# Another group spilled through DRAM, sums of squares by transfers, and two merged VectorE operations in a gated linear attention with a mixture of experts

## The chip, the core and the metric

The kernel runs on one core of one Trainium2 chip. A core has TensorE (PE, matrix products, with its weight loads listed as PEld), VectorE (DVE), ScalarE (ACT), GpSimd (POOL) and SyncE (SP), each with an instruction stream of its own that is worked off in order; they meet at semaphores. Transfers are issued from SP's queue or from GpSimd's and are carried out by 16 DMA engines. The metric is the device time of one execution in microseconds (us). Lower is better.

## The reference

A linear attention with complex decay per channel (4 batches, 8 heads, 768 positions, 48 channels), followed by a layer of 8 experts of which each token uses at most one.

```python
mag = np.sqrt(a_re * a_re + a_im * a_im)
scale = np.minimum(mag, 0.999) / (mag + 1e-06)
a_re_n, a_im_n = (a_re * scale, a_im * scale)
for t in range(S):
    ar, ai = (a_re_n[:, :, t, :, None], a_im_n[:, :, t, :, None])
    new_re = ar * S_re - ai * S_im
    new_im = ar * S_im + ai * S_re
    S_re, S_im = (new_re + kv, new_im)          # kv = k[t] outer v[t]
    y[:, :, t] = np.einsum('bhd,bhde->bhe', q[:, :, t], S_re)
...
do_compute = x @ w_skip > 0                     # x: y as 3072 tokens of 384
e_idx = np.argmax(xc @ w_gate, axis=1)          # gate_w: softmax at e_idx
h = np.maximum(xc[mask] @ w1[e], 0.0)
y[mask] = gate_w[mask, None] * (h @ w2[e])
out[do_compute] = xc + y
```

## The kernel before, in words

**Tiling.** The 768 positions are 6 chunks of 128, taken as 3 groups of two. Within a chunk, products of the decay factors run outwards from the middle, backwards in one half and forwards in the other, so that 128 partitions hold (half, chunk, batch and head) and a group needs 64 steps and one at the end. The state of a step, `W`, is a complex product over 48 channels. A group is 8 pieces of 8 steps.

**The recurrence** (`chain`) takes two VectorE operations a step: `X` (L371), the four real products, and the next `W` (L380). Each depends on the one before, and other VectorE work is placed between them.

**A gate** (`gate`, with `scale`) prepares the factors of one piece, two pieces ahead. `ain` holds the imaginary part in column 0, the real part in column 1 and the negated imaginary part in column 2. ScalarE squares the two parts (L258), VectorE adds them (L262), ScalarE makes the scale `t` by logarithm and exponential (L263 to L267, with one VectorE operation, L266). Then VectorE multiplies the imaginary part by `t` and a sign that is -1 on the second half of the partitions (L316), ScalarE writes the negated copy (L321), and VectorE multiplies the real part by `t` (L324). GpSimd sets the few rows at a group's ends.

**A piece is consumed** (`consume`): ScalarE squares `W` (L438), VectorE forms `nw`, a query or key times `W` (L443); the two squares are added by two TensorE products with the identity into a bank of PSUM (L452, tile `sw`), or on VectorE in the last piece of a group (L457); ScalarE takes logarithm and exponential (L459, L460), VectorE refines the reciprocal (L462, L464), applies it (L467) and forms `iw` (L470). In groups that stay on the chip, TensorE transposes `nw` and `iw` (L533) and ScalarE copies the result into `qk` (L540), 16 transposes and 8 copies a piece. `keep` (L492) sends what is needed in natural layout to DRAM (`kq`), from GpSimd's queue: half of it for a group that stays, all of it for the group that is spilled. The last piece of the kernel goes through `final` instead.

**The spilled group** is group 1 (`spilled`). Its transposes are not made in `consume`; each of its units loads keys and queries from `kq` (`nat`, L503; for the others only keys, L506) and `turn` transposes them, 16 transposes (L518) and 4 copies (L520).

**A unit** (`unit_at`, `unit`) is the attention of one chunk and one batch, eight units a group: products of keys and queries (L590, tiles `pa`, two of one bank each), the mask on VectorE (L612, one operation a bank), the state between chunks (L625 to L663), the output products (L667, L670), their transposition (L675), and the scores of the router. The next unit's L590 is issued in the middle of a unit, before its output products. Units of group g run during the recurrence of group g+1; those of group 2 run after it.

**Order.** `Order` is a planner that fixes the program order: it steps generators by priority (units, router, consume, gates, weights) between the steps of the recurrence, with costs and due times of its own. A unit may start only at a given step (`PACE`), a piece of the recurrence only when the piece three before it is consumed, and the pieces of group 2 behind the first only after 8 units, since `qk` has two buffers a group and group 2 takes those of group 0. The scheduler below it works with simulated times; `issue_after` pins the masks behind a step of the recurrence.

**The end.** Router and scatter (L739) bring the tokens of each expert together in DRAM (`xs`); then eight experts run on TensorE, each with two layers in split precision (L1000 to L1028).

Of the kernel before, what the change touches and what calls it, by code (L numbers as in the profile page):

```python
# [9 lines left out]
F32 = mybir.dt.float32  # L10
# [3 lines left out]
AF = mybir.ActivationFunctionType  # L14
ALU = mybir.AluOpType
AX = mybir.AxisListType
PSUM = bass.MemoryType.PSUM
DRAM = bass.MemoryType.DRAM

B, H, S, D = 4, 8, 768, 48  # L20
DM = H * D
BH = B * H
C = 128
HC = 64
NCH = S // C
NG = NCH // 2
# [73 lines left out]
def vt(n, f=1.0):  # L100
    return (n / f + 65) / 0.96
# [8 lines left out]
class Kern:  # L110
# [12 lines left out]
    def consts(self, ctx):  # L123
# [26 lines left out]
        self.sgn = col[:, 0:1]  # L150
        g.memset(self.sgn[0:64], 1.0)
        g.memset(self.sgn[64:128], -1.0)
# [149 lines left out]
    def gate(self, g, p):  # L302
        nc = self.nc
        V, A = nc.vector, nc.scalar
        n = LP + (1 if p == NP - 1 else 0)
        i = g * NP + p
        if i == 0:
            self.load_a(0)
        if i + 1 < NPC:
            self.load_a(i + 1)  # L310
        ain = self.ain[i]
        last = i == NPC - 1
        t = yield from (self.scale_last if last else self.scale)(i, n, ain)
        N = n * D
        o = self.order
        V.scalar_tensor_tensor(ain[:, :, 0], ain[:, :, 0], self.sgn, t, ALU.mult, ALU.mult)  # L316
        if p == 0:
            nc.gpsimd.memset(ain[0:64, 0, 0], 0.0)
        if n > LP:
            nc.gpsimd.memset(ain[64:128, LP, 0], 0.0)  # L320
        A.activation(ain[:, :, 2], ain[:, :, 0], AF.Copy, scale=-1.0)  # L321
        self.ready[i] = o.act(N, 1, o.t + vt(N))
        yield vt(N), 0
        V.tensor_tensor(ain[:, :, 1], ain[:, :, 1], t, ALU.mult)  # L324
        if p == 0:
            nc.gpsimd.memset(ain[0:64, 0, 1], 1.0)
        if n > LP:
            nc.gpsimd.memset(ain[64:128, LP, 1], 1.0)
        yield vt(N), 0
        self.gates_done = i + 1  # L330
# [10 lines left out]
    def chain(self, g):  # L341
        V = self.nc.vector
        qk = None
        if not self.spilled(g):
            qk = [self.qkp.tile([96, BH, 4, HC], F32, name=f"qk_{g}_{cc}", tag="qk") for cc in range(2)]
# [43 lines left out]
    def consumers(self):  # L389
        while self.cons_done < NPC:  # L390
            g, u = divmod(self.cons_done, NP)
            if self.cq and (self.spilled(g) or u < 1 or self.units_done >= (g - 1) * 2 * B):
                yield from self.consume(*self.cq.pop(0))
            else:
                yield 0, 100

        self.rctx.close()
        self.m0 = self.pool(self.mctx, "m0", side="right")
        self.mr = self.pool(self.mctx, "mr", 2, side="right")
        self.t2 = self.pool(self.mctx, "t2", side="right")  # L400
        self.order.add(P_WEIGHTS, self.weights(0, self.m0), 3000)
# [30 lines left out]
    def consume(self, g, i, W, num, inv, jb, qk, wl):  # L432
# [16 lines left out]
        if wl is None:  # L449
            sw = self.ps_w.tile([128, LP, D], F32, name=f"sw_{i}", tag="sw")  # L450
            for c in range(2):
                nc.tensor.matmul(sw, self.ident, ws[:, :, c], start=(c == 0), stop=(c == 1))  # L452
            o.pe(1300, ts)
            cost = 0.0
        else:
            sw = w2
            V.tensor_tensor(w2, w2, r0, ALU.add)  # L457
            cost = vt(N)
# [12 lines left out]
        tq = self.trans(i, iw, 2, 1, jb, qk, vt(2 * N)) + 5000  # L471
# [12 lines left out]
    def spilled(self, g):  # L484

        return g == 1
# [8 lines left out]
    def nat(self, c, b):  # L495

        if c >= 2 * (NG - 1):
            return
        g, cc = divmod(c, 2)
        t = self.nats[c, b] = self.un.tile([C, H, 2, 2 * D], F32, name=f"nat_{c}_{b}", tag="nat")  # L500
        r = cc * BH + b * H
        if self.spilled(g):
            self.nc.sync.dma_start(t.rearrange("p h q d -> p (h q) d"),  # L503
                                   self.kq[g][r:r + H].rearrange("h q s d -> s (h q) d"))
        else:
            self.nc.sync.dma_start(t[:, :, 0], self.kq[g][r:r + H, 0].rearrange("h s d -> s h d"))  # L506

    def turn(self, c, b):
# [3 lines left out]
        qk = self.un.tile([96, H, 4, HC], F32, name=f"qkT_{c}_{b}", tag="qkT")  # L512
# [65 lines left out]
    def unit_at(self, c, b):  # L578
# [9 lines left out]
        pa = [self.ps_at.tile([128, 4, C], F32, name=f"pa_{c}_{b}_{hh}", tag="pa") for hh in range(2)]  # L588
        for h in range(H):
            nc.tensor.matmul(pa[h // 4][:, h % 4], KT(h), QT(h), start=True, stop=True)  # L590
# [8 lines left out]
    def unit(self, c, b):  # L599
# [9 lines left out]
        for hh in range(2):  # L609

            with self.tc.issue_after(self.cins):
                V.tensor_tensor(at[:, hh * 4:hh * 4 + 4], pa[hh],  # L612
                                self.mask.rearrange("p (o t) -> p o t", o=1).to_broadcast([128, 4, C]), ALU.mult)
            yield o.wait(vt(512), 0 if hh == 0 or c == 0 else self.rx_t)
# [76 lines left out]
        nx = c * B + b + 2  # L691
# [12 lines left out]
    def units(self, g):  # L704
        self.nat(2 * g, 0)
        self.nat(2 * g, 1)
# [172 lines left out]
    def attention(self):  # L879
        with ExitStack() as ctx:  # L880
# [4 lines left out]
            self.qkp, self.un, self.st = P("qk", 2), P("un", 2), P("st")  # L885
            self.ps_tp, self.ps_at = P("ps_tp", 2, space=PSUM), P("ps_at", 2, space=PSUM)
# [359 lines left out]
```

## Time and profile before

| | |
|---|---|
| median of 3 runs | 538.61 us (535.48 to 540.12) |
| profiled execution | 543.87 us |
| its span, first to last instruction | 542.2 us |
| mean granted clock of TensorE | 0.887 |
| HBM read, written | 61.84 MB, 25.21 MB |

The profile is of one execution, and its time is outside the range of the three timed runs. A row of a group of instructions gives line, engine, operation, written and read tiles, shape and count; behind the first bar the busy time in us and the mean of one in ns; behind the second the idle time of the engine just before them and what ended it. A row of a stretch gives its length, then busy us and instructions of each engine, TensorE's granted clock, the DMA share and GB/s. A row of waits gives who waited for whom, us in total, times, and the longest. A row in order of time gives start, duration, engine, line and shape, and how many like it are merged. A row of a transfer gives KB each and the median us from issue to landing. Busy time of TensorE is not time at its peak, and idle time of an engine that does not bound a stage costs nothing.

### The profile page before, as it was taken

The numbers are of one execution on the slowest core, as the hardware profiler recorded it, in microseconds if no ns is written. First come the engines' busy times: TensorE is split into PE (matmuls) and PEld (weight loads), VectorE is DVE, ScalarE is ACT, GpSimd is POOL, SyncE is SP. The second block draws the span as 40 slices with busy tenths as digits, with TensorE's granted clock in tenths as the row PEclk, the third lists the DMA queues.
The fourth block names the chain that finished last, engine by engine and source line by source line (L and its number), as shares of the span: only waits on it lengthen the run. The fifth ranks groups of instructions, "written<-read, shape, count | busy, mean of one in ns | idle before, by whom it ended". The sixth has DMA issues, their size and how long they took to land. (4 is left out here: it accounts for less than half of the span.)

```text
span 542.2 us, 10042 instructions
## 1 busy us (share of the span) xinstructions
PE 430.7 (79%) x3253; PEld 376.9 (70%) x3253; DVE 412.1 (76%) x1139; ACT 291.8 (54%) x658; POOL 88.3 (16%) x158
## 2 busy tenths in 40 slices
PE   0256446579989322899999998999998999999994
PEld 0134324479866201788778888998988999999994
DVE  2988999965999989789889847689469566866621
ACT  3657657714655554587778673332266454654410
POOL 4011011101132444000000300202112001120111
PEclk9966876667999765799999996799999999999998
DMA  4558777787988867858644325534659568666300
GB/s 85 113 113 179 176 151 169 159 163 178 230 196 195 197 152 168 186 113 194 135 112 110 96 67 179 145 113 119 219 175 312 189 209 273 182 196 226 105 20 28
DMA packets 160523, 85.72 MB, mean 158 GB/s; under 512 B 134491, under 2 KB 154463, under 8 KB 160464
## 3 DMA queue, kind: packets, MB, share of 16 engines
q1 hardware_dynamic: 155216, 70.93, 51.7%
q0 software_dynamic: 5248, 14.07, 9.6%
q8 instruction: 28, 0.46, 0.3%
q14 instruction: 31, 0.25, 0.1%
HBM read 61.84 MB, written 25.21 MB: 161 GB/s over the span
## 5 line engine op out<-in xcount | busy, mean ns | idle before, releaser
L452 PE MATMUL sw<-ws,ident 128*128 128x384 f32 x84 | 44.3, 664 | 37.9 <-ACT ws L438 37.9
L371 DVE TENSOR_TENSOR X<-W,ain 128x192 f32<-128x192 f32 x192 | 67.7, 352 | 2.9
L936 DVE TENSOR_TENSOR l<-r,h 128x768 fp32r<-128x768 f32 (+1 forms) x56 | 58.0, 1069 | 13.3 <-ACT h L935 13.2
L935 ACT CAST h<-r 128x768 fp32r<-128x768 f32 (+1 forms) x56 | 49.7, 925 | 17.6 <-DMA r<-in_moe_w_dram 12.7
L452 PEld LDWEIGHTS sw<-ws,ident 128*128 128x128 f32 x84 | 19.5, 257 | 50.6 <-issue 27.1
L1000 PE MATMUL ph<-xh,h 128*128 128x256 f32 x192 | 53.0, 282 | 0.6 <-issue 0.6
L1000 PE MATMUL ph<-xh,l 128*128 128x256 f32 x192 | 53.2, 282 | 0.0
L1002 ACT ACTIVATE hh<-ph 128x256 fp32r<-128x256 f32 x64 | 23.7, 382 | 53.8 <-PE ph L1000 53.8
L612 DVE TENSOR_TENSOR at<-pa,mask 128x512 f32<-128x512 f32 x48 | 32.7, 685 | 25.1 <-PE pa L590 21.4
L380 DVE TENSOR_TENSOR W<-X 128x96 f32<-128x96 f32 x192 | 48.7, 254 | 3.4
L1000 PE MATMUL ph<-xl,h 128*128 128x256 f32 x192 | 51.0, 281 | 0.0
L533 PE MATMUL tp<-ident,iw 128*96 128x128 f32 x128 | 23.6, 331 | 33.6 <-DVE iw L470 33.3
L1003 DVE SCALAR_TENSOR_TENSOR hl<-ph,hh 128x256 fp32r<-128x256 f32 x64 | 25.6, 418 | 29.2 <-ACT hh L1002 29.2
L540 ACT COPY qk<-tp 96x256 f32<-96x256 f32 x128 | 39.8, 369 | 11.4 <-PE tp L533 10.9
L1023 PE MATMUL po<-h,hh 128*128 128x384 f32 x128 | 43.8, 342 | 0.0
L739 POOL DMA_INDIRECT xs<-xa,sl x24 | 29.1, 1212 | 88.8 <-DVE l L936 20.5
L533 PEld LDWEIGHTS tp<-ident,iw 128*96 128x96 f32 x128 | 17.1, 151 | 37.9 <-issue 30.6
L1024 PE MATMUL po<-l,hh 128*128 128x384 f32 x128 | 43.3, 338 | 0.0
L667 PE MATMUL py<-at,vt 128*64 128x128 f32 x384 | 42.5, 298 | 0.0
L590 PE MATMUL pa<-qk 96*128 96x128 f32 x256 | 41.3, 316 | 1.0 <-DVE at L612 0.9
L1025 PE MATMUL po<-h,hl 128*128 128x384 f32 x128 | 39.5, 337 | 0.0
L590 PEld LDWEIGHTS pa<-qk 96*128 96x128 f32 x256 | 36.9, 222 | 3.2 <-PE py L670 1.1
(225 smaller groups left out, 1077.2 us busy)
## 6 DMA issues: line engine op xcount, KB each, us to landing
r<-in_moe_w_dram SPq DMA_DIRECT2D x24, 512.0 KB, 5.4
r<-in_moe_w_dram SPq DMA_DIRECT2D x32, 384.0 KB, 4.2
nat<-kq SPq DMA_DIRECT2D x8, 768.0 KB, 5.5
kq<-nw POOLq DMA_DIRECT2D x24, 192.0 KB, 3.4
kq<-iw POOLq DMA_DIRECT2D x24, 192.0 KB, 2.9
vt<-in_v_dram SPq DMA_DIRECT2D x24, 192.0 KB, 2.8
out_dram<-xa SPq DMA_DIRECT2D x24, 192.0 KB, 2.1
ain<-in_a_re_dram SPq DMA_DIRECT2D x90, 48.0 KB, 2.9
```

What stands on the lines that cost most here:

```text
L371: V.tensor_tensor(X, prev.unsqueeze(1).to_broadcast([128, 2, 2, D]), windows(ain[:, j]), ALU.mult)
L380: self.cins = V.tensor_tensor(W[:, j, ::-1], X[:, :, 0], X[:, :, 1], ALU.add).ins
L452: nc.tensor.matmul(sw, self.ident, ws[:, :, c], start=(c == 0), stop=(c == 1))
L533: nc.tensor.transpose(tp[:, jj], src[:, s * 4 + jj], self.ident)
L540: nc.scalar.copy(o, tp[:, :, :, cc].rearrange("p j s b -> p b s j"))
L590: nc.tensor.matmul(pa[h // 4][:, h % 4], KT(h), QT(h), start=True, stop=True)
L667: PE.matmul(py[j * 64:j * 64 + 64, hp], vt_[:, 2 * hp + j], at[:, 2 * hp + j], start=True, stop=(c == 0))
L935: nc.scalar.copy(hi[:, ks], raw)
L936: nc.vector.tensor_tensor(lo[:, ks], raw, hi[:, ks], ALU.subtract)
L1000: pe = PE.matmul(ph, w[:, k, js], x[:, k], start=(n == 0), stop=(n == len(terms) - 1))
L1023: PE.matmul(po, hh[:, j, sl], w2h[:, j], start=(j == 0), stop=False)
L1024: PE.matmul(po, hh[:, j, sl], w2l[:, j], start=False, stop=False)
```

## The change

Group 0 is spilled instead of group 1. The `qk` pool has three buffers: one for group 0, which holds its loads (`nat`) and turned tiles as parts of one area, and two for each of groups 1 and 2 in turn; a piece of group 2 behind the first is consumed only after 12 units. For group 1, the keys are loaded into one buffer, one unit ahead instead of two. Units of a group that is not spilled may start 5 us earlier in the planner's time.

In groups 1 and 2 the two squares are added by an accumulating transfer within SBUF, from GpSimd's queue, in place of TensorE's two products (and VectorE's sum in the last piece of group 1). Group 0 keeps TensorE's sums.

In a gate, ScalarE first negates the imaginary part on the second half of the partitions, in place; then one VectorE operation multiplies both parts by `t`. The negated copy follows it. In a unit, `pa` is one tile of two banks and the mask one operation; the pool has one buffer of it instead of two.

```diff
+        A.activation(ain[64:128, :, 0], ain[64:128, :, 0], AF.Copy, scale=-1.0)
+        o = self.order
+        o.act(n * D)
         t = yield from (self.scale_last if last else self.scale)(i, n, ain)
-        V.scalar_tensor_tensor(ain[:, :, 0], ain[:, :, 0], self.sgn, t, ALU.mult, ALU.mult)
+        V.tensor_tensor(ain[:, :, 0:2], ain[:, :, 0:2], t.unsqueeze(2).to_broadcast([128, n, 2, D]), ALU.mult)
...
-        A.activation(ain[:, :, 2], ain[:, :, 0], AF.Copy, scale=-1.0)
-        V.tensor_tensor(ain[:, :, 1], ain[:, :, 1], t, ALU.mult)
+        A.activation(ain[:, :, 2], ain[:, :, 0], AF.Copy, scale=-1.0)
...
-            qk = [self.qkp.tile([96, BH, 4, HC], F32, name=f"qk_{g}_{cc}", tag="qk") for cc in range(2)]
+        qk = [self.qkp.tile([128, BH * 4 * HC], F32, name=f"qk_{g}_{cc}", tag="qk")
+              for cc in range(1 if self.spilled(g) else 2)]
+        if self.spilled(g):
+            self.area, qk = qk[0], None
...
-            if self.cq and (self.spilled(g) or u < 1 or self.units_done >= (g - 1) * 2 * B):
+            if self.cq and (g < NG - 1 or u < 1 or self.units_done >= 3 * B):
...
-        if wl is None:
+        if g:
+            sw = w2
+            nc.gpsimd.dma_start(w2, r0, accum_op=ALU.add)
+            ts += 4000
+            cost = 0.0
+        elif wl is None:
...
-        tq = self.trans(i, iw, 2, 1, jb, qk, vt(2 * N)) + 5000
+        tq = self.trans(i, iw, 2, 1, jb, qk, vt(2 * N)) + 5000 * self.spilled(g)
...
-        return g == 1
+        return g == 0
...
-        t = self.nats[c, b] = self.un.tile([C, H, 2, 2 * D], F32, name=f"nat_{c}_{b}", tag="nat")
         if self.spilled(g):
+            t = self.part(c, b, 0, H * 4 * D).rearrange("p (h q d) -> p h q d", h=H, q=2)
...
         else:
+            t = self.un.tile([C, H, 1, 2 * D], F32, name=f"kt_{c}_{b}", tag="kt", bufs=1)
...
+    def part(self, c, b, o, n):
+        o += (c * B + b) % 2 * n
+        return self.area[:, o:o + n]
...
-        qk = self.un.tile([96, H, 4, HC], F32, name=f"qkT_{c}_{b}", tag="qkT")
+        qk = self.part(c, b, 2 * H * 4 * D, H * 4 * HC)[0:96].rearrange("p (h k t) -> p h k t", h=H, k=4)
...
-        pa = [self.ps_at.tile([128, 4, C], F32, name=f"pa_{c}_{b}_{hh}", tag="pa") for hh in range(2)]
+        pa = self.ps_at.tile([128, H, C], F32, name=f"pa_{c}_{b}", tag="pa")
...
+            V.tensor_tensor(at, pa, self.mask.rearrange("p (o t) -> p o t", o=1).to_broadcast([128, H, C]), ALU.mult)
...
-        nx = c * B + b + 2
+        nx = c * B + b + (2 if self.spilled(c // 2) else 1)
...
-            self.qkp, self.un, self.st = P("qk", 2), P("un", 2), P("st")
-            self.ps_tp, self.ps_at = P("ps_tp", 2, space=PSUM), P("ps_at", 2, space=PSUM)
+            self.qkp, self.un, self.st = P("qk", 3), P("un", 2), P("st")
+            self.ps_tp, self.ps_at = P("ps_tp", 2, space=PSUM), P("ps_at", 1, space=PSUM)
```

More of the change, by code (lines that the diff above doesn't have):

```diff
@@ L149, in consts @@
         col = cst.tile([128, 8], F32, name="col")
-        self.sgn = col[:, 0:1]
-        g.memset(self.sgn[0:64], 1.0)
-        g.memset(self.sgn[64:128], -1.0)
         self.lnb = col[:, 1:2]
@@ L320, in gate @@
             nc.gpsimd.memset(ain[64:128, LP, 0], 0.0)
[L321 to L324, printed above, removed]
+            nc.gpsimd.memset(ain[64:128, LP, 1], 1.0)
         if p == 0:
             nc.gpsimd.memset(ain[0:64, 0, 1], 1.0)
-        if n > LP:
-            nc.gpsimd.memset(ain[64:128, LP, 1], 1.0)
-        yield vt(N), 0
+        A.activation(ain[:, :, 2], ain[:, :, 0], AF.Copy, scale=-1.0)
+        self.ready[i] = o.act(N, 1, o.t + vt(2 * N))
+        yield vt(2 * N), 0
         self.gates_done = i + 1
@@ L342, in chain @@
         V = self.nc.vector
-        qk = None
-        if not self.spilled(g):
-            qk = [self.qkp.tile([96, BH, 4, HC], F32, name=f"qk_{g}_{cc}", tag="qk") for cc in range(2)]
+        qk = [self.qkp.tile([128, BH * 4 * HC], F32, name=f"qk_{g}_{cc}", tag="qk")
+              for cc in range(1 if self.spilled(g) else 2)]
+        if self.spilled(g):
+            self.area, qk = qk[0], None
+        else:
+            qk = [t[0:96].rearrange("p (h k t) -> p h k t", h=BH, k=4) for t in qk]
         self.QK[g] = qk
@@ L587, in unit_at @@
         nc.sync.dma_start(vt_[:, :, 0:D], self.v3[b * H:b * H + H, c * C:c * C + C, :].rearrange("h s d -> s h d"))
-        pa = [self.ps_at.tile([128, 4, C], F32, name=f"pa_{c}_{b}_{hh}", tag="pa") for hh in range(2)]
+        pa = self.ps_at.tile([128, H, C], F32, name=f"pa_{c}_{b}", tag="pa")
         for h in range(H):
-            nc.tensor.matmul(pa[h // 4][:, h % 4], KT(h), QT(h), start=True, stop=True)
+            nc.tensor.matmul(pa[:, h], KT(h), QT(h), start=True, stop=True)
         self.pa[c, b] = pa
@@ L608, in unit @@
         pa = self.pa.pop((c, b))
[L609 to L614, printed above, removed]
+        with self.tc.issue_after(self.cins):
+            V.tensor_tensor(at, pa, self.mask.rearrange("p (o t) -> p o t", o=1).to_broadcast([128, H, C]), ALU.mult)
+        yield o.wait(vt(1024), 0 if c == 0 else self.rx_t)
         late = self.last(c)
@@ L705, in units @@
         self.nat(2 * g, 0)
-        self.nat(2 * g, 1)
+        if self.spilled(g):
+            self.nat(2 * g, 1)
         self.unit_at(2 * g, 0)
```

2 lines of the change are left out of this document (1 added, 1 removed).

## The prediction

> **What bounds the kernel now.** I read the page first, then the busy time by stage, then the waits of VectorE, and last single instructions in order of time. The page's chain of waits is of no use here (it stops after two pieces, 0.1% of the span), so the bound is read stage by stage. I cut the span where the recurrence of a group ends: the first step starts at 12.2, the last piece's sum on VectorE (L457) marks the ends of groups 0 and 1 at about 95 and 203.7, and the last step ends at about 311. From 311 to 325 the last transposes run, then eight late units to 384.6, then the experts.
>
> ```profile
> span 542.2 us, 10042 instructions
> L371 DVE TENSOR_TENSOR X<-W,ain x192: 343/351/360, 12.2 to 309.9; 128x192 f32<-128x192 f32 x192
> 94.51 0.55 DVE L457 TENSOR_TENSOR ws<-ws 128x384 f32<-128x384 f32 x1
> 203.53 0.55 DVE L457 TENSOR_TENSOR ws<-ws 128x384 f32<-128x384 f32 x1
> core 0: us, PE busy (x) PEld busy (x) DVE busy (x) ACT busy (x) POOL busy (x), PEclk, DMA share, GB/s
> 12.20:95.00 82.80, 40.64 (x144) 26.85 (x145) 75.34 (x201) 54.50 (x137) 10.26 (x20) 0.75 0.70 149
> 95.00:203.70 108.70, 76.53 (x582) 62.24 (x580) 92.92 (x273) 56.14 (x132) 27.46 (x44) 0.80 0.80 184
> 203.70:311.00 107.30, 96.61 (x771) 77.49 (x773) 93.74 (x262) 74.19 (x181) 10.62 (x14) 0.90 0.62 140
> 311.00:325.00 14.00, 13.31 (x134) 11.52 (x130) 6.71 (x24) 10.52 (x33) 1.18 (x2) 1.00 0.25 65
> 325.00:384.60 59.60, 57.54 (x584) 54.19 (x585) 47.17 (x209) 19.69 (x40) 9.54 (x10) 0.89 0.50 147
> 384.60:542.20 157.60, 146.08 (x1047) 144.65 (x1045) 93.84 (x172) 71.44 (x130) 22.70 (x27) 0.99 0.54 176
> ```
>
> The reader is to see that VectorE carries stages 0 to 2 (91%, 85% and 87% busy), TensorE everything after. Idle VectorE is 7.5, 15.8 and 13.6 us. Where it sits, and what ended it, shorter stretches and the waits in each stage say:
>
> ```profile
> 110.00:120.00 10.00, 8.76 (x54) 7.68 (x55) 4.86 (x13) 1.33 (x3) 0.07 (x1) 0.61 0.77 133
> 120.00:130.00 10.00, 10.00 (x55) 9.18 (x55) 5.62 (x15) 2.85 (x6) 2.40 (x4) 0.54 0.85 220
> 150.00:160.00 10.00, 8.47 (x71) 6.78 (x73) 9.74 (x42) 6.92 (x16) 3.83 (x6) 1.00 0.98 219
> 180.00:190.00 10.00, 1.82 (x12) 0.88 (x10) 10.00 (x43) 4.93 (x12) 4.24 (x8) 0.70 0.80 191
> 220.00:230.00 10.00, 9.24 (x53) 8.45 (x52) 6.69 (x15) 5.17 (x9) 0.00 (x0) 0.66 0.81 158
> 260.00:270.00 10.00, 10.00 (x79) 7.79 (x77) 7.70 (x17) 9.11 (x23) 0.00 (x0) 1.00 0.62 144
> DVE sq L266 <- ACT t L264: 4.2, 7, 1.3
> DVE at L612 <- PE pa L590: 10.6, 5, 3.4
> DVE at L612 <- PE pa L590: 5.3, 7, 3.1
> ```
>
> The three wait rows are of stages 0, 1 and 2. In stage 1, 9.5 of the 15.8 idle us lie between 110 and 130: the first units of group 0 begin there, TensorE runs at a granted clock of 0.61 and 0.54, and VectorE stands before the mask until the attention products are there. At 180 TensorE has almost nothing to do (1.82 of 10) and VectorE is full. In stage 2 it is the other way: TensorE is at 10.00 of 10 and VectorE at 7.70.
>
> **The change part by part.** The sum is against the profiled execution, 543.9 us with a span of 542.2; that is 1.0% above the median of 538.6, so the result is scaled by 538.61/543.87 = 0.990.
>
> ```profile
> L316 DVE SCALAR_TENSOR_TENSOR ain<-ain,col,t 128x384 f32<-128x384 f32 (+1 forms) x24 | 14.9, 620 | 2.5 <-ACT t L267 1.7
> L324 DVE TENSOR_TENSOR ain<-ain,t 128x384 f32<-128x384 f32 (+1 forms) x24 | 13.3, 556 | 0.0
> L443 DVE TENSOR_TENSOR nw<-num,W 128x768 f32<-128x768 f32 x23 | 21.9, 953 | 1.6 <-PE tp L533 1.3
> L612 DVE TENSOR_TENSOR at<-pa,mask 128x512 f32<-128x512 f32 x48 | 32.7, 685 | 25.1 <-PE pa L590 21.4 <-PE py L667 3.5
> L321 ACT ACTIVATE ain<-ain 128x384 f32<-128x384 f32 (+1 forms) x24 | 12.7, 528 | 2.9 <-POOL ain L320 1.4 <-DVE ain L316 1.2 <-POOL ain L318 0.2
> L540 ACT COPY qk<-tp 96x256 f32<-96x256 f32 x128 | 39.8, 369 | 11.4 <-PE tp L533 10.9 <-PE pr L772 0.4
> L520 ACT COPY qkT<-tu 96x512 f32<-96x512 f32 x32 | 18.1, 583 | 7.7 <-PE tu L518 7.7
> ```
>
> Gate products: two operations of 620 and 556 ns become one over 768 elements, which costs 953 ns in the row of that shape. That saves 0.22 us a gate, 1.8 us in each of the three stages. The sign moves to a new ScalarE operation ahead of each gate, priced as L321 at 528 ns: 4.2 us of ScalarE a stage. The two sign memsets of GpSimd go, worth nothing. At the very start nothing covers the new operation: 0.53 us for it, and the last gate copy now waits for 953 ns instead of running beside the second product, so +0.8 us.
>
> Masks: from 384 to 768 elements an operation grows by 0.40 us (556 to 953), so 1024 elements take 685 + 0.53 = 1.22 us against 2 x 0.685: 0.15 us a unit, 1.2 us in each of stages 1 and 2. Against it, the mask now waits for all eight products instead of four, and the next unit's products wait for the whole mask, because one score buffer of double size replaces two. In the late units, at 97% TensorE, I take +1 us (0 if scheduled around; 8 x 0.7 = 6 if each unit exposes it).
>
> What moves between the stages is TensorE and ScalarE work:
>
> ```profile
> 303.80 1.04 PE L518 MATMUL tu<-ident,nat 128*96 128x128 f32 x8
> 307.33 0.60 PE L533 MATMUL tp<-ident,nw 128*96 128x128 f32 x4
> 231.45 1.46 PE L452 MATMUL sw<-ws,ident 128*128 128x384 f32 x4
> 212.77 0.84 ACT L438 ACTIVATE ws<-W 128x768 f32<-128x768 f32 x1 [2.93 <-DVE W L380]
> 216.69 0.56 ACT L459 ACTIVATE ws<-sw,col 128x384 f32<-128x384 f32 x1
> L492 POOL DMA_DIRECT2D kq<-nw x24 | 15.7, 659 | 35.0 <-DVE X L371 27.7 <-DVE W L380 5.1 <-DVE rk L789 2.2
> kq<-nw POOLq DMA_DIRECT2D x24, 192.0 KB, 3.4
> nat<-kq SPq DMA_DIRECT2D x8, 768.0 KB, 5.5
> nat<-kq SPq DMA_DIRECT2D x8, 384.0 KB, 5.3
> q0 software_dynamic: 5248, 14.07, 9.6%
> DMA to landing us min/median/max: 2.6/3.5/8.2
> DVE ws L462 <- ACT ws L460: 1.1, 2, 0.9
> ```
>
> A piece's 16 direct transposes cost 4 x 0.60 = 2.4 us of TensorE, 19 us a group, and half of L540, 19.9 us, of ScalarE. A unit's 16 turning transposes cost 2.1 us, 17 us a group, and 18.1 us of ScalarE. A piece's sum costs 1.5 us at full clock; 14 go (7 in each of stages 1 and 2), 10 us a stage. One VectorE sum of 0.55 us goes in stage 1. So the stages get:
> - Stage 0: TensorE 40.6 - 19 = 22, ScalarE 54.5 - 19.9 + 4.2 = 39.
> - Stage 1: TensorE 76.5 + 19 + 17 - 10 = 102, ScalarE 56.1 + 19.9 + 18.1 + 4.2 = 98.
> - Stage 2 with the 14 us behind it: TensorE 109.9 - 17 - 10 = 83, ScalarE 84.7 - 18.1 + 4.2 = 71.
>
> Queues: 16 spills go from stage 1 to stage 0, with 0.66 us of GpSimd each. All software transfers take 9.6% of the DMA engines for at most 88 issues, so at most 0.6 us each at all sixteen: the DMA share of stage 0 rises from 0.70 to about 0.82. At 0.98 between 150 and 160 VectorE was 97% busy, so I cost that at nothing. SP's loads of a group's keys double in stage 1 (768 KB for 384 KB, 0.2 us more to land) and halve in stage 2. There a single buffer lets a load start only after the unit before has used it; 5.3 us against one unit in some 12 us of stage 2 covers it. Behind a late load TensorE stands with the next products, and behind them the mask. The new transfers wait in GpSimd's queue for the square on ScalarE; what stands behind them is spills and scatters, which nobody awaits soon.
>
> Sum by transfer: not shown by this trace. Today the logarithm starts 3.1 us after the square ends (213.61 to 216.69). A transfer of the same 192 KB needs its issue, taken as 0.7 us, and 3.4 us to land: 4.1. The bounds go from -3 us for a group (the row's 2.6 us landing beats a queued TensorE) to 8.2 us a landing. I take nothing for it, since VectorE waited for this path only 1.1 us in all of stage 1.
>
> The terms:
> - Start: +0.8.
> - Stage 0: VectorE -1.8; its waits for ScalarE (4.2 us) fall by 1.5 as ScalarE is emptier: -3.3.
> - Stage 1: VectorE -1.8, -1.2, -0.5. The first unit now needs a load and a turn, as group 1's has now, where 220 to 230 lost 3.3 us: so 6 of the 9.5 idle us go. But TensorE stands at 102 and ScalarE at 98 of some 105 us: I add 5 us of waits, what stage 2 lost from 230 to 311 beyond its start being 10. Sum -4.5.
> - Stage 2: VectorE -3.0, TensorE waits -3, and +2 since the pieces of group 2 behind the first now wait for twelve units instead of eight. Sum -4.
> - 311 to 325: TensorE was 95% busy with units that lagged; 27 us less of it ahead. -4 (0 to -9).
> - Late units: +1. Experts: 0.
>
> Together -14: 543.9 - 14 = 530, times 0.990 gives 525 us.
>
> The clock at the start of the units is a matter of its own. In the rows it stays at 0.54 while TensorE is busy 10.00 of 10. By the Trainium skill (TensorE: Matmul & The Clock Gate, The HAM clock gate) about 3.4 us of sustained work would bring it back; by that the start would lose under 2 us and the sum would be 2 us better. The trace does not agree: 20 us there at about half.
>
> **The rivals.**
> - Slower: ScalarE becomes the bound of stage 1. Its 98 us today never run denser than 9.11 of 10, where VectorE falls to 7.70, and 69% over stage 2. The other terms give -9, so the change loses once stage 1 is over 118 us, that is once ScalarE runs there below 83%. At 75% stage 1 takes 131 us, +22: 543.9 + 13 = 557, scaled 551. Against it: units can run over into stage 2, where ScalarE has room.
> - No change: the transfers come later than the sums and nothing hides it. 14 x 1.0 us eats the 14: 544, scaled 539. A late twelfth unit would give about the same. For it: the order on VectorE is fixed, so a late operand stops the recurrence behind it. By the Trainium skill (DMA: Bandwidth & Descriptors, Anatomy of one DMA) a software transfer takes about 2.0 us plus its bytes over 436e3, an estimate of 2.5 us for 196608 bytes, and this rival would cost 14 x 0.1 = 1.4 us. The trace does not agree: its row has 3.4 us for those bytes.
> - Faster than forecast: the three engines fit. If VectorE runs at 95% in stages 1 and 2, as from 150 to 190 now, they take 89.4/0.95 = 94 and 90.7/0.95 = 95.5, -26 in place of -8.5, and the tail loses 9: about 506, scaled 502.
>
> **How the numbers follow.** Forecast 0.52; faster still 0.10; no change 0.20; slower 0.18. A measurement of this kernel tells about 1% from no change, so faster is 0.62, within 1% 0.20, slower 0.18. The forecast's own range is 513 to 533. The range 507 to 546 leaves out about half of the slowest and of the fastest case.
>
> **What would show it.** In the changed profile: one product of about 0.95 us a gate and one mask of about 1.22 us a unit; stage 0 near 79.5 us, stage 1 near 104, stage 2 near 103, the stretch to the first late unit near 10. TensorE near 22 in stage 0 and at full clock in most of stage 1. If stage 1 is longer than 109 with ScalarE over 90 us, the first rival holds; if VectorE waits for the second logarithm's result in most pieces, the second. What would make it wrong at once is a wait inside the buffer that loads and turned tiles now share, which would chain each unit's load to the last unit's end.

## The result and the profile after

The changed kernel takes 566.88 us (median of 4 runs, 564.84 to 568.86) against 539.37 us (535.48 to 544.68) for the kernel before on the same chip: a ratio of 1.053, interval 1.046 to 1.061. It is slower by 5.3%. The forecast was 525 us with a range of 507 to 546. The profiled execution, 568.86 us, has a span of 567.1. Ratios go by fast runs alone, while the profiled executions of the kernel before and, further down, of both_merges, tiny_twice and two_ws were slow ones of their kernels (543.87, 561.22, 571.46 and 547.65 us), so their rows show where time goes and not the exact size of a difference.

I read the changed profile in the same order. First the busy time by stage, cut at the same places: the first step, the first step of groups 1 and 2, the last step. Each row has the stretch and its length, then busy us of TensorE, weight loads, VectorE, ScalarE and GpSimd with their instructions, the granted clock, the DMA share and GB/s.

```profile
core 0: us, PE busy (x) PEld busy (x) DVE busy (x) ACT busy (x) POOL busy (x), PEclk, DMA share, GB/s
0.00:13.70 13.70, 0.00 (x0) 0.00 (x0) 2.65 (x6) 6.36 (x11) 6.27 (x42) 1.00 0.47 85
13.70:99.70 86.00, 20.46 (x28) 8.22 (x28) 77.68 (x196) 48.74 (x101) 19.38 (x35) 0.64 0.75 176
99.70:214.30 114.60, 86.82 (x759) 75.63 (x759) 87.02 (x226) 82.40 (x197) 26.72 (x33) 0.87 0.93 186
214.30:345.30 131.00, 95.30 (x778) 80.45 (x779) 101.75 (x302) 74.97 (x199) 33.13 (x27) 0.82 0.61 112
345.30:567.10 221.80, 207.20 (x1634) 201.44 (x1633) 139.48 (x365) 93.44 (x177) 27.72 (x35) 0.95 0.52 164
```

The same cuts in the kernel before (12.6, 95.0, 204.0, 311.1 of 542.2) give a start of 12.6 us and these rows:

```profile
12.60:95.00 82.40, 40.64 (x144) 26.85 (x145) 74.98 (x200) 54.50 (x137) 10.26 (x20) 0.75 0.70 150
95.00:204.00 109.00, 76.53 (x582) 62.24 (x580) 93.22 (x274) 56.44 (x133) 27.76 (x44) 0.80 0.80 184
204.00:311.10 107.10, 96.71 (x773) 77.59 (x775) 93.54 (x263) 73.99 (x180) 10.41 (x14) 0.90 0.62 139
311.10:542.20 231.10, 216.84 (x1762) 210.26 (x1756) 147.62 (x402) 101.56 (x202) 33.32 (x39) 0.96 0.51 162
```

So the start lost 1.1, stage 0 3.6, stage 1 5.6 and stage 2 23.9 us, and everything behind the last step gained 9.3: +24.9 in all. VectorE did less (408.6 us over the span against 412.1), but stood idle 27.6 us in stage 1 and 29.3 us in stage 2, where the kernel before had 15.8 and 13.6. ScalarE, which one rival feared for stage 1, is busy 82.4 of 114.6 us and does not bound it.

What VectorE waited for, first in stage 1, then in stage 2 (who waited for whom, us in total, times, longest):

```profile
DVE at L624 <- PE pa L603: 12.1, 5, 6.2
DVE ws L468 <- ACT ws L466: 2.2, 2, 1.8
...
DVE ws L468 <- ACT ws L466: 11.6, 7, 3.0
DVE iw L476 <- PE tp L546: 3.8, 1, 3.8
```

L468 is the product with what ScalarE makes of the sum by a logarithm (L465) and an exponential (L466); the prediction and the expectations call it the second logarithm's result. In the kernel before, VectorE's wait for it (L462) was 1.1 us in stage 1; now it comes late seven times in stage 2. The operations that touch a piece's squares (the tile `ws`), with durations in ns as least, median and most, then first and last start, then how long engines stood until a transfer was there, and the time from the issue of one to its landing:

```profile
L438 ACT ACTIVATE ws<-W x23: 826/843/911, 20.3 to 329.7; 128x768 f32<-128x768 f32 x23
L465 ACT ACTIVATE ws<-ws,col x16: 607/615/663, 100.0 to 336.3; 128x384 f32<-128x384 f32 x16
L452 POOL DMA_DIRECT2D ws<-ws x15: 1547/1603/1701, 107.6 to 330.8; - x15
...
  DMA ws<-ws: 23.1, 10
...
DMA to landing us min/median/max: 5.4/5.5/7.2
```

There are 15 transfers, each with 1.60 us on GpSimd; the six whose landing the trace shows land 5.5 us (median) after the start of their issue. The 1.60 us are part of the 5.5: the shortest way from the end of a square to the logarithm among the 15 pieces is 5.7 us, less than 1.60 + 5.5. ScalarE stands before the logarithm (L465) for 23.1 us in ten of them, and VectorE behind ScalarE for 2.2 + 11.6 = 13.8 us in nine. Where the prediction read 3.1 us from the end of the square to the logarithm in one piece of the kernel before, the mean over the 15 pieces of the later groups is 4.29 us there and 7.83 us here. The page's row of the software queue (packets, MB, share of 16 engines) shows what a transfer loads:

```profile
q0 software_dynamic: 20848, 17.02, 15.9%
```

Before it was 5248 packets and 9.6% of 542.2 us: (0.159 x 567.1 - 0.096 x 542.2) / 15 = 2.5 us of all sixteen engines for each transfer, and 15600 / 15 = 1040 packets.

The rows for the merges are as forecast, 967 ns for a product, 1220 for a mask, 525 for the new negation, and the last waits 24.2 us for a gate's loads (in the kernel before the square behind it, L258, waited 29.9 us for loads, 12.4 of them a gate's):

```profile
L624 DVE TENSOR_TENSOR at<-pa,mask 128x1024 f32<-128x1024 f32 x24 | 29.3, 1220 | 24.2 <-PE pa L603 21.6 <-PE py L678 2.5
L316 DVE TENSOR_TENSOR ain<-ain,t 128x768 f32<-128x768 f32 (+1 forms) x24 | 23.2, 967 | 3.3 <-ACT t L264 2.1 <-DMA ain<-in_a_im_dram 0.6
L310 ACT ACTIVATE ain<-ain 64x384 f32<-64x384 f32 (+1 forms) x24 | 12.6, 525 | 24.5 <-DMA ain<-in_a_im_dram 24.2
```

### The profile page after: what moved, and what is told of

It is laid out like the page before. It is cut to its first block, busy times and chain, and to the rows that moved or that the text cites. A ratio compares the mean times of both kernels' runs of the same rounds, so it can differ in the third digit from the quotient of the medians.

```text
span 567.1 us, 9920 instructions
## 1 busy us (share of the span) xinstructions
PE 409.8 (72%) x3197; PEld 365.7 (64%) x3197; DVE 408.6 (72%) x1090; ACT 305.9 (54%) x682; POOL 113.2 (20%) x171
## 5 line engine op out<-in xcount | busy, mean ns | idle before, releaser
L458 PE MATMUL sw<-ws,ident 128*128 128x384 f32 x28 | 20.5, 886 | 68.9 <-ACT ws L438 68.9
L603 PE MATMUL pa<-qk 96*128 96x128 f32 x384 | 58.8, 310 | 2.3 <-DVE at L624 1.9
L458 PEld LDWEIGHTS sw<-ws,ident 128*128 128x128 f32 x28 | 8.2, 324 | 80.0 <-ACT ws L438 54.5
L603 PEld LDWEIGHTS pa<-qk 96*128 96x128 f32 x384 | 53.9, 221 | 5.6 <-DVE at L624 3.2
L751 POOL DMA_INDIRECT xs<-xa,sl x24 | 31.3, 1303 | 123.5 <-DVE W L380 30.6
L624 DVE TENSOR_TENSOR at<-pa,mask 128x1024 f32<-128x1024 f32 x24 | 29.3, 1220 | 24.2 <-PE pa L603 21.6
L546 PE MATMUL tp<-ident,iw 128*96 128x128 f32 x128 | 22.3, 317 | 32.0 <-DVE iw L476 23.4
L1037 PE MATMUL po<-h,hl 128*128 128x384 f32 x128 | 39.8, 340 | 0.0
```

Of the source, the lines that this page charges most:

```text
L546: nc.tensor.transpose(tp[:, jj], src[:, s * 4 + jj], self.ident)
L603: nc.tensor.matmul(pa[:, h], KT(h), QT(h), start=True, stop=True)
L1037: pe = PE.matmul(po, hl[:, j, sl], w2h[:, j], start=False, stop=(j == NF - 1))
```

## The experiments

Ratios are to the kernel before, run on the same chip, with 95% intervals.

### One part undone or alone

**The sums back on TensorE** (u_sums), and only that:

```diff
-        if g:
-            sw = w2
-            nc.gpsimd.dma_start(w2, r0, accum_op=ALU.add)
-            ts += 4000
-            cost = 0.0
-        elif wl is None:
+        if wl is None:
```

> The changed kernel with the sums of squares of groups 1 and 2 back on TensorE; the rest of the change stays. If the transfers are the cause (theory A: VectorE waits 15.8 us for them, and they load the DMA engines with some 38 us), the time falls from 567 to 548 or less, and VectorE's wait for the second logarithm falls under 3 us. If the order of the groups is the cause (theory B: the recurrence stands because transposes wait for the buffers of units that still run), it stays at 555 to 562, with the recurrence of group 2 still over 120 us long.

544.82 us, 1.016 (1.006 to 1.026). Against the changed kernel some 20 us come back by the ratios, 22 between the medians: the transfers are the main cause. The other half of the expectation failed. VectorE's wait for the second logarithm does not fall under 3 us; in groups 1 and 2 it is

```profile
DVE ws L462 <- ACT ws L460: 12.1, 4, 6.2
```

against 13.8 us in nine pieces of the changed kernel. So this row does not measure what the transfers cost. What falls is VectorE's idle time in stages 1 and 2 as a whole, from 56.8 to 40.2 us, and no single row has it.

**The transfers alone** in the kernel before (only_transfers), the same lines the other way round:

> The kernel before with nothing but the sums of groups 1 and 2 by transfers. Theory A: 550 to 560, with VectorE waiting over 10 us for the second logarithm. Theory B: 537 to 545.

560.67 us, 1.043 (1.033 to 1.053), 23 us; VectorE's wait for the second logarithm is 18.7 us. The two agree within their intervals, so no strong dependence of the cost on the other parts is seen.

**The group order undone** (u_group):

```diff
-            if self.cq and (g < NG - 1 or u < 1 or self.units_done >= 3 * B):
+            if self.cq and (g < NG - 1 or u < 1 or self.units_done >= 2 * B):
...
-        return g == 0
+        return g == 1
```

> The changed kernel with the middle group spilled again, and group 2 waiting for eight units as before; transfers and merged operations stay. Theory A: 555 to 562, the transfers' wait stays near 15 us. Theory B: 548 or less, and the recurrence of group 2 back to about 110 us.

574.68 us, 1.069 (1.057 to 1.082), above both expectations. Undoing it makes things no better and, by the medians, 8 us worse, so the new order is not what costs; the two intervals overlap. **Alone** in the kernel before (only_swap: `spilled`, with the buffers and the delay that go with it):

> The kernel before with the first group spilled instead of the middle one and nothing else. From the two pairs run so far (574.7 to 566.9 and 551.3 to 544.8): 529 to 533. If swapping only helped because the merged mask was there, 537 or more.

537.67 us, 1.003 (0.998 to 1.007): nothing that can be told, and not the gain that the first half of its expectation forecast. **With the gate's merge** (swap_gate: two masks, sums on TensorE):

> The first group spilled and the gate products merged; two masks on two score buffers, sums on TensorE. If the gains add up (first group spilled: 6 to 8 us, measured by undoing it), C1 expects 525 to 532, faster than both kernels. C2 expects 538 to 545.

542.52 us, 1.009 (1.004 to 1.013): no gains that add up.

**The merges one by one** in the kernel before. The gate's single product with its negation (only_gate), and the single mask on one score tile of double size, in a pool of one buffer (only_mask):

```diff
+        A.activation(ain[64:128, :, 0], ain[64:128, :, 0], AF.Copy, scale=-1.0)
...
-        V.scalar_tensor_tensor(ain[:, :, 0], ain[:, :, 0], self.sgn, t, ALU.mult, ALU.mult)
...
-        V.tensor_tensor(ain[:, :, 1], ain[:, :, 1], t, ALU.mult)
+        V.tensor_tensor(ain[:, :, 0:2], ain[:, :, 0:2], t.unsqueeze(2).to_broadcast([128, n, 2, D]), ALU.mult)
```

> The kernel before with the merged gate product alone (ScalarE negates first). Theory C1 (the one mask and the one score buffer cost what the merged version loses): 531 to 536, a gain of some 5 us. Theory C2 (the negation ahead of every gate makes the gates late): 543 to 552, with more VectorE waits for the gate's logarithm and exponential.

```diff
-        pa = [self.ps_at.tile([128, 4, C], F32, name=f"pa_{c}_{b}_{hh}", tag="pa") for hh in range(2)]
+        pa = self.ps_at.tile([128, H, C], F32, name=f"pa_{c}_{b}", tag="pa")
...
-                V.tensor_tensor(at[:, hh * 4:hh * 4 + 4], pa[hh],
-                                self.mask.rearrange("p (o t) -> p o t", o=1).to_broadcast([128, 4, C]), ALU.mult)
+            V.tensor_tensor(at, pa, self.mask.rearrange("p (o t) -> p o t", o=1).to_broadcast([128, H, C]), ALU.mult)
```

> The kernel before with the merged mask alone, one score tile of two banks in one buffer. C1: 545 to 555, with the late units some 8 us longer and VectorE waiting longer in front of the mask. C2: 531 to 536.

534.09 us, 1.001 (0.997 to 1.006), and 535.32 us, 0.998 (0.992 to 1.004). Both times lie where a gain was expected, but on this chip the kernel before takes 534.11 us, so there is none. By the rows of the two kernels the gates save 14.9 + 13.3 - 23.2 = 5.0 us of VectorE and the masks 32.7 - 29.3 = 3.4, and neither can be seen in the time. Neither merge harms alone.

### What of the merges and the leftovers costs 2.5%

**Transfers and group order both undone** (merges). Left are the merges, a third area buffer, one key buffer for the resident groups, and no planned delay of 5 us before their units:

> Both undone: of the change only the merged gate product, the merged mask with its one score buffer, and the single key buffer are left. Both theories expect 530 to 537, the gain of the 9 us of VectorE that the merges save. If it is not faster than 539, the merges cost as much as they save, and that is a third cause (theory C: one mask behind eight products, and one score buffer).

551.3 us, 1.025 (1.012 to 1.038), though neither merge alone costs anything. Three runs part what is left: the two merges in the kernel before and nothing else (both_merges); merges with `+ 5000 * self.spilled(g)` back at `+ 5000` (merges_5000); that one edit the other way in the kernel before (delay_by_group); and a fourth puts the delay back in u_sums (sums_5000).

> The kernel before with the gate's merged product and the unit's single mask, and nothing else of the change. Each alone changed nothing (1.0013 and 0.9976). Theory I (the two merges hurt together: with one score buffer a unit's scores wait for the mask of the unit before, and a gate's product of 0.97 us in one piece is what that mask waits behind): 1.015 to 1.025, stages 0 and 2 longer, some 88 and 109 us as in the kernel with both undone. Theory L (they do no harm; the 2.5% of the kernel with the transfers and the group order undone come from what was left beside the merges: one key buffer for the resident groups, and their units released 5 us of planned time earlier): 0.990 to 1.003, stage 0 near 82.

> The kernel with the transfers and the group order undone (551.3, 1.025), with one thing more undone: the 5 us of planned delay before the first unit of a group is there for all groups again, so the merges, the single key buffer and the third area buffer are left. Theory I: unchanged, 1.02 to 1.03. Theory L by the delay: near 1.00, the stretch between the chains (21 us) and stage 0 (88.5 us) as before. Theory L by the key buffer: unchanged, 1.02 to 1.03, so this run and the one with the merges alone tell the three apart.

> The kernel before with one edit: the 5 us of planned delay before a group's units only for the spilled group, as in the changed kernel. All work is the same. Theory D: 1.015 to 1.025, lost after the last step of the recurrence, where the kernel with the merges lost 17 us (243.5 against 226.2 from the last W to the end). Theory O: not the same loss in the same place; within 1% or a loss elsewhere.

> The changed kernel with the sums back on TensorE (544.8, 1.016) and with the 5 us of planned delay for all groups again. Theory D (the delay's removal has a cost of its own): 0.99 to 1.005, as it was with the other group order (1.025 to 1.001). Theory O (the order that comes out of the planner by chance decides; small edits move the time by 1 to 3% either way): anywhere from 0.99 to 1.03, with no part of the trace that changes alike in both pairs.

both_merges 1.027 (1.017 to 1.037), merges_5000 1.001 (0.997 to 1.006), delay_by_group 0.994 (0.990 to 0.999), sums_5000 1.010 (1.006 to 1.014). No single suspect fits. The merges together cost 2.7% in one kernel and nothing in another that holds them too; putting the delay back is worth 2.4% in one pair and 0.6% in another, where the intervals overlap, and in the third kernel taking it away costs nothing. Theory I had both_merges right, its stages too (88.8 and 108.9 us), and falls with merges_5000, theory L with both_merges and theory D with delay_by_group; of those stated only theory O is left, that the order which comes out decides, and its expectation was so wide that to fit it proves little. What speaks for it is in the traces. These edits move instructions far from where they are made. The kernels merges and merges_5000 do the same work and differ in nothing but a planned delay, that is in the order: by source lines, 702 of 1091 VectorE instructions stand in matching stretches, and the time differs by 2.4%. In the same way it is 852 of 1091 in both_merges and merges_5000. Two places show what such a loss looks like. In both_merges stage 1 is 115.4 us, with VectorE idle for 10.7 of them in one go (start, duration, engine, line; in brackets the idle time before and what ended it):

```profile
149.30 0.56 ACT L313 ACTIVATE ain<-ain 64x432 f32<-64x432 f32 x1 [6.26 <-DMA ain<-in_a_im_dram]
149.88 0.58 ACT L459 ACTIVATE ws<-sw,col 128x384 f32<-128x384 f32 x1
151.17 0.51 ACT L460 ACTIVATE ws<-ws 128x384 f32<-128x384 f32 x1
...
140.65 0.36 DVE L371 TENSOR_TENSOR X<-W,ain 128x192 f32<-128x192 f32 x1
151.72 0.56 DVE L462 TENSOR_TENSOR ws<-sw,ws 128x384 f32<-128x384 f32 x1 [10.71 <-ACT ws L460]
```

The new negation (L313) is ScalarE's first work on a gate. Here it waits for a load at the head of the queue, as the square behind it does in the kernel before, the logarithm and the exponential of another piece behind it (L459, L460) wait too, and VectorE waits for them. That another order would have avoided this stop is argued, not shown. In the kernel merges the loss lies behind the last step, 243.5 us against 226.2 in merges_5000. Two windows of merges there:

```profile
340.00:350.00 10.00, 6.41 (x56) 5.76 (x57) 6.10 (x21) 4.42 (x8) 1.97 (x2) 0.77 0.40 140
350.00:360.00 10.00, 10.00 (x56) 9.85 (x57) 4.76 (x23) 1.55 (x4) 3.12 (x4) 0.50 0.29 84
```

TensorE loses 3.59 us in one window, and its clock is 0.50 in the next. From 330 to the end of the late units, first merges, then merges_5000:

```profile
330.00:393.00 63.00, 56.11 (x557) 51.94 (x557) 44.71 (x192) 17.74 (x37) 9.01 (x10) 0.86 0.42 118
330.00:376.00 46.00, 45.45 (x531) 42.59 (x530) 39.64 (x179) 16.23 (x35) 10.10 (x10) 1.00 0.55 158
```

For nearly the same number of products merges has 10.7 us more of TensorE's busy time, at a clock of 0.86 instead of 1.00, and 6.3 us more of its idle time.

### What of a transfer costs 23 us

Two explanations were open: its load (2.5 us of all DMA engines, 1.6 us of GpSimd) or the wait for it.

**The same transfers into a buffer that nobody reads**, sums on TensorE (idle_transfers), and **the real transfers with the consumer giving way** for 6 us of planned time (deferred_transfers, its diff against only_transfers):

```diff
+            if g:
+                nc.gpsimd.dma_start(self.idle, r0, accum_op=ALU.add)
```

> The kernel before, its sums still on TensorE, and besides for each of the 15 pieces of the later groups the same accumulating transfer of 192 KB, into a buffer that nobody reads. Nothing waits for it but the next one and the buffer it reads. Theory load (the 2.5 us of all 16 DMA engines and the 1.6 us on GpSimd per transfer, 38 and 24 us in all, delay the loads and the kept halves): 1.03 or more, most of the 23 us of the kernel with the real transfers. Theory wait (what costs is that the logarithm and VectorE's product stand behind 7 us of issue and landing): 0.998 to 1.012.

```diff
-            ts += 4000
+            yield o.wait(0, o.t + 6000)
             cost = 0.0
```

> The kernel before with the transfers in groups 1 and 2, and with the planner told: after issuing a transfer the consumer gives way for 6 us of planned time, so the logarithm is issued behind other ScalarE work and VectorE gets other work meanwhile. Theory wait, by the head of the queue: most of the 23 us comes back, 1.000 to 1.015, the wait for the second logarithm under 5 us in all. Theory wait, by the recurrence (a piece ends 6 us later whoever is told, and its buffers and transposes come later): 1.02 to 1.045, the wait gone from the logarithm and turned into one for the products' buffers and the masks. Theory load: 1.03 or more too, told apart by the run with the idle transfers.

555.1 us, 1.032 (1.024 to 1.040), which looked like load; 561.46 us, 1.045 (1.038 to 1.051), so telling the planner gives nothing back, and ScalarE still waits 17.3 us for the transfers. In idle_transfers, and in the three later runs that keep TensorE's sums, the last piece of group 1 has no transfer, so there are 14 and not the 15 of the expectations. And idle_transfers did not part load and wait. Two of its wait rows:

```profile
ACT ws L461 <- DMA idle<-ws: 14.3, 7, 4.6
ACT ws L438 <- DVE inv L469: 8.8, 7, 2.3
```

The logarithm writes the half of the squares that the transfer reads, so it waited all the same. The next pair repairs that. **The load without the wait** (free_transfers) takes `W` as the source; **a wait without the load** (tiny_transfers) lets the logarithm's result go to a buffer of its own, into which a transfer of one step comes first (24 KB, which is 1/8 of the bytes and not the 1/16 of its expectation):

```diff
+            if g:
+                nc.gpsimd.dma_start(self.idle, Wm[:, :, 0], accum_op=ALU.add)
```

> The kernel before, its sums on TensorE, and besides one accumulating transfer of 192 KB for each of the 15 pieces of the later groups, from the chain's result W (three buffers) into a buffer that nobody reads, so that no logarithm waits for it. Theory load: 1.03, as the idle transfers gave. Theory wait: 0.998 to 1.010, and the wait of VectorE for the second logarithm back at what the kernel before has (under 4 us, from 15.8).

```diff
+            if g:
+                nc.gpsimd.dma_start(self.lr[:, LP - 1], r0[:, LP - 1], accum_op=ALU.add)
+                r0 = self.lr
```

> The kernel before, its sums on TensorE, and the logarithm's result in a buffer of its own, into which an accumulating transfer brings one step of the squares (1/16 of the bytes) first, so that the logarithm of the later groups waits for a transfer that is almost no load. Theory wait: 1.02 to 1.04, with ScalarE waiting some 10 us or more for the transfers. Theory load: 0.998 to 1.010.

541.6 us, 1.004 (0.998 to 1.009), and 538.16 us, 0.994 (0.990 to 0.998). The load alone, 14 transfers of it, costs nothing that can be told, and VectorE's wait for the second logarithm is 4.3 us (under 4 was expected). The tile's view in free_transfers shows that it was really there:

```profile
L455 POOL DMA_DIRECT2D idle<-W x14: 1537/1614/1670, 103.1 to 295.0; - x14
DMA to landing us min/median/max: 5.3/6.6/8.5
```

The tiny wait was too short to judge, for ScalarE stood before it only 2.5 us in all. So **the tiny transfer twice** (tiny_twice), the line above repeated, and, the other way round, **a second buffer for the squares** beside the real transfers (two_ws, made on only_transfers):

```diff
-        ws = self.wk.tile([128, LP, 2, D], F32, name=f"ws_{i}", tag="ws", bufs=1)
+        ws = self.wk.tile([128, LP, 2, D], F32, name=f"ws_{i}", tag="ws", bufs=2)
```

> The kernel with the tiny transfers, each of them made twice, one after the other, so that the logarithm of a later group starts some 8 to 9 us after its squares, as late as with the real transfers, at 1/8 of their load. Theory wait (the length decides, and the first microseconds are free because TensorE's sums and ScalarE's other work take as long): 1.02 to 1.045. Theory both (only a wait that the loaded engines lengthen in single pieces, and loads that come late beside it, cost): 0.995 to 1.012.

> The kernel before with the transfers in groups 1 and 2 (560.7, 1.043), and two buffers in place of one for the squares, so that the next piece's squares need not wait for VectorE's product with the sum (5.6 us of ScalarE's waits, three times). Theory one buffer: most of the loss goes, 1.00 to 1.015. Theory wait by the order of the queues (the logarithm stands at the head of ScalarE's queue, the product at the head of VectorE's, whatever buffers there are): 1.03 to 1.045.

tiny_twice: 567.82 us, 1.044 (1.032 to 1.057). two_ws: 542.71 us, 1.005 (0.999 to 1.010). In tiny_twice, a quarter of the bytes (its expectation says 1/8) and sums on TensorE give the waits of the real transfers in smaller number:

```profile
ACT lr L463 <- DMA lr<-ws: 10.5, 5, 5.9
DVE at L616 <- PE pa L594: 18.7, 10, 5.8
DVE ws L466 <- ACT lr L464: 13.2, 7, 7.4
```

The table has the gap from the end of the square to the logarithm (mean of 15 pieces in groups 1 and 2) and VectorE's idle time, the length of stages 1 and 2 less its busy time in the rows by stage:

| kernel | gap, us | VectorE idle, us | ratio |
|---|---|---|---|
| before | 4.29 | 29.3 | 1 |
| free_transfers | 4.16 | 29.6 | 1.004 |
| tiny_transfers | 5.83 | 22.6 | 0.994 |
| idle_transfers | 8.60 | 42.0 | 1.032 |
| only_transfers | 8.14 | 53.7 | 1.043 |
| deferred_transfers | 8.57 | 53.8 | 1.045 |
| tiny_twice | 9.47 | 46.0 | 1.044 |
| two_ws | 8.94 | 39.8 | 1.005 |
| u_sums | 3.61 | 40.2 | 1.016 |
| changed kernel | 7.83 | 56.8 | 1.053 |

Among the kernels that change nothing but this path, with one buffer a mean gap up to 5.8 us goes with no loss and one of 8.1 us or more with a loss of 3 to 4.5%, whatever the load; with two buffers a gap of 8.9 us goes with none that can be told. The order of VectorE's instructions, compared with that of the kernel before as above, does not sort them so: in matching stretches stand 918 of 1139 in free_transfers, 928 in tiny_transfers, 925 in tiny_twice, which loses 4.4%, and 729 in two_ws, which loses nothing. That is against the order as the cause of these losses, though a count of stretches can't exclude it; in only_transfers it is 655, so part of its 23 us may be order. The rows by stage for stages 1 and 2, first of only_transfers, then of two_ws:

```profile
95.30:209.50 114.20, 81.32 (x556) 71.49 (x554) 93.26 (x282) 56.12 (x134) 36.45 (x42) 0.62 0.86 174
209.50:335.60 126.10, 89.86 (x747) 74.77 (x748) 93.33 (x248) 74.15 (x176) 30.25 (x31) 0.81 0.76 143
```

```profile
94.80:197.80 103.00, 81.15 (x554) 71.78 (x552) 89.33 (x267) 54.10 (x127) 32.80 (x44) 0.63 0.95 194
197.80:319.70 121.90, 91.80 (x745) 76.72 (x745) 95.81 (x262) 75.87 (x183) 31.36 (x29) 0.81 0.76 146
```

Stage 1 is 11.2 us shorter with the second buffer, stage 2 4.2 us; the spans differ by 18.2 us, the medians by 18.0. The transfers and their place in GpSimd's queue are the same in both. The waits in both stages, first of only_transfers, then of two_ws:

```profile
ACT ws L465 <- DMA ws<-ws: 24.6, 10, 4.8
ACT ws L438 <- DVE inv L473: 5.6, 3, 2.9
DVE ws L468 <- ACT ws L466: 18.7, 9, 4.5
```

```profile
ACT ws L465 <- DMA ws<-ws: 11.1, 7, 4.2
DVE ws L468 <- ACT ws L466: 10.5, 6, 3.0
```

With one buffer the squares of the next piece wait for VectorE's last use of the buffer (L438 for L473), and only then can their transfer start: each late piece hands its delay on. With two that row is gone and the waits for the transfers fall by about half, though a transfer lands no earlier (a median of 7.2 us against 6.7). That the delay is handed on is a reading of these rows: the row that goes is 5.6 us, and the gain is 18. Three things stay open. In the changed kernel itself L438 waits for `W` (8.7 us) and never for that use, so there the one buffer is not seen at work as a wait. The order also differs between the two (923 of 1138 VectorE instructions stand in matching stretches), so part of the gain may be order; 23 us becoming 2 or 3 is more than any run moved in which order is the only suspect left (some 14 us). And the second buffer was not tried in the changed kernel. No kernel beats the one before by as much as the 1% that can be told.

## Why the prediction was wrong

**The step that failed** is "Sum by transfer", which ends "I take nothing for it, since VectorE waited for this path only 1.1 us in all of stage 1". The term at nothing measured some 20 us in the changed kernel (u_sums) and 23 in the kernel before (only_transfers). That is half of the miss: 1.053 measured against a forecast of 525/538.6 = 0.975 is 42 us. The other half is that the gain of 14 us did not come and some 8 us (u_sums, 1.6%) were lost besides, which the other terms below answer as far as is known. Three things in the step were wrong.
- Its price: a row's landing counts from the start of the issue, so 0.7 + 3.4 = 4.1 us counts the issue twice, and the spills' rows give 3.4. The new transfer took 5.5. The spills were near in bytes and far in kind: the new one stays within SBUF, runs in stretches of 192 bytes and adds into its destination. Which of the three makes it take longer no run shows.
- Its cover: a short wait of VectorE before the change says that the result came in time, not by how much. By the means the slack was some 1.5 us at least (a gap of 5.83 was as free as one of 4.29), and less than 3.5. Over 15 pieces 7.83 - 4.29 = 3.5 us are 53 us of lateness, of which the time shows some 20.
- Its bound: the step put "8.2 us a landing" as the upper end and did not carry it into the range. By that end a piece is 8.2 - 3.1 = 5.1 us later, 71 us for 14 pieces (there were 15); a third of it on the path would have taken the forecast from 525 to some 548, beyond the range.

**The "no change" rival had the mechanism.** It has the transfers come later than the sums with nothing to hide it, and the late operand stop the recurrence. Its sign, VectorE's wait for the second logarithm in most pieces, is there in nine of the fifteen with a transfer, but it is a weak sign: u_sums has 12.1 us of the same wait without a transfer. Its price of 1.0 us a piece was too small; u_sums and only_transfers put it at 1.3 to 1.5 us a piece (20 and 23 us over 15). That the squares have a single buffer stood in the code and was not in the prediction.

**The other terms**, from the two profiled executions:
- Start, +0.8: +1.1.
- Stage 0, -3.3: +3.6. TensorE's size held (20.5 us for the 22 forecast), ScalarE's did not (48.7 for 39). Ten gates' products fall in this stage instead of eight, and ten of the sums ahead of them instead of nine, some 2 x (0.56 + 0.97) + 0.56 = 3.6 us of VectorE that stage 1 then lacks. A stage's length is no measure of what an edit saved when work moves over its end.
- Stage 1, -4.5: +5.6, and stage 2, -4: +23.9. In u_sums, without the transfers, they are 108.0 and 118.3 us, -1.0 and +11.2, and what is behind the last step is 16.3 us less, so there stage 2's growth is late work done earlier (its rows from stage 1 on):

```profile
100.00:208.00 108.00, 90.93 (x751) 75.30 (x751) 86.53 (x229) 81.67 (x198) 15.41 (x26) 0.91 0.79 184
208.00:326.30 118.30, 100.03 (x832) 81.28 (x833) 99.59 (x299) 73.98 (x195) 16.37 (x17) 0.89 0.48 110
326.30:541.10 214.80, 202.13 (x1644) 195.54 (x1642) 140.40 (x367) 94.84 (x183) 29.75 (x36) 0.98 0.53 170
```

- TensorE and ScalarE in stage 1, forecast at 102 and 98 us: 86.8 and 82.4. The work ran over into stage 2, as the prediction said against its slower rival.
- The stretch behind stage 2 and the late units, -4 and +1: -9.3 with the experts, at the far end of the bound of "0 to -9" given for the first.
- The savings of VectorE were costed as savings of time. Of the 8.4 us that the two merges take from VectorE, only_gate and only_mask show nothing. A reading, not a finding: the waits in these stages end with a load, with ScalarE or with TensorE, and a shorter operation only meets them earlier.

**The slower rival** named the wrong engine. ScalarE was to bound stage 1 at 83% or less of more than 118 us; the stage took 114.6 us. ScalarE's longest waits in stages 1 and 2 were those for the transfers, 23.1 us in ten, which it did not have before.

**"A wait inside the area buffer"** is there (TensorE before a turn waited twice for a load into it, 10.5 us in all), but is not decisive: the new group order alone, with that buffer, costs 0.3%.

About 1.6% of the 5.3% (u_sums) is not the transfers. It isn't settled on one part: the runs with and without the delay, the order and the merges spread from 0.994 to 1.027 with no constant effect of any. That an order alone can lose this much merges and merges_5000 show (2.4% for the same work); which stops make up u_sums's 1.6% is open.

## What to carry to other kernels

Before a short engine sum is exchanged for a transfer, count the buffers that hold its operands: here the same transfers cost 23 us with one buffer and nothing that can be told with two. Test such a loss by its halves, the load without the wait and the wait without the load, and see in the trace whether the wait is really gone in the test. And in a kernel whose order a planner writes, run an edit of no work as a control before a change of two per cent is put down to its idea.

## What the runs showed of the hardware

- An accumulating transfer of 192 KB between two halves of a tile, in runs of 192 bytes, held GpSimd 1.60 us and landed 5.4 to 7.2 us after the start of its issue in the changed kernel. By the Trainium skill (DMA: Bandwidth & Descriptors, Anatomy of one DMA) a software transfer of these bytes is an estimate of 2.5 us; the trace does not agree, by a factor of two and more. At 1/8 of the bytes it took 0.91 us of GpSimd and 3.6 us to land in tiny_transfers, so most of the landing is not the bytes.
- In the windows of merges above, TensorE ran a full 10 us at a clock of 0.50 with no idle time, after losing 3.6 us in the window ahead. By the Trainium skill (TensorE: Matmul & The Clock Gate, The HAM clock gate) some 3.4 us of work would bring the clock back; the trace does not agree, as in the kernel before (0.54 in a window of 10 us with TensorE busy for all of it). A stop of 3.6 us on TensorE was so followed by a stretch of work at half the clock.
